# Column halves in the last matmul chain of an attention and mixture kernel, a last weight in four pieces, and short products between the weights

## The chip, the cores and the metric

The kernel runs on one core of a Trainium2 chip. The metric is the device time of one execution in microseconds. A core has a matrix engine (TensorE, PE in the profile), which writes its products into PSUM banks, a vector engine (VectorE, DVE), a scalar engine (ScalarE, ACT), a third elementwise engine (GpSimd, POOL), and a sync engine (SyncE, SP), from which this kernel issues every transfer between device memory (DRAM) and the on-chip memory. All of them run on their own and wait for each other by semaphores; each takes its own instructions strictly in the order in which they were written.

## What is computed

Cut to what matters (the inputs are float32; the norm guards of 1e-9 are left out here):

```python
a      = softmax(phi, axis=memories)          # 8 batches, 8 heads, 576 positions, 32 memories
k_m    = einsum('bhsm,bhsd->bhmd', a, k)      # keys and values pooled into 32 memories
v_m    = einsum('bhsm,bhsd->bhmd', a, v)
x      = softmax(q @ k_m.T / 8) @ v_m         # as rows: 4608 x 512
logits = x @ moe_phi                          # 4608 x 32 slots
slot_input = softmax(logits, axis=rows).T @ x # 32 x 512, four slots for each of 8 experts
for e in range(8):
    h = relu(slot_input[e] @ w1[e])           # first layer:  4 x 512 @ 512 x 1024
    slot_out[e] = h @ w2[e]                   # second layer: 4 x 1024 @ 1024 x 512
out = softmax(logits, axis=slots) @ slot_out  # 4608 x 512
```

The change touches the second layer, the sum that follows it, and the first rows of the last product.

## The kernel before

Until about two thirds of the time the kernel works on attention: four pairs of batches, one after another, whose logits are kept, and whose slot inputs are added up. When the last pair is done, the slot inputs are scaled into the tile `SIM` (L1000), and the mixture begins.

**First layer.** `expert_in` multiplies each expert's slot inputs with its `w1`, which arrives as two transfers of 1 MB. Four experts share a PSUM bank, and four products of 32 columns of the array each run side by side (`tile_position`). After four experts `hidden` applies the relu (L1080), turns the result by two transposes (L1089) and stores it as `hT` (L1095).

**Second layer.** `expert_out` takes each `w2` as two transfers of 1 MB, called halves here: 16 halves in all. A half is four products with 512 columns each (L1113), again side by side on four quarters of the array. All 64 products add up in one accumulator, `pacc`, in the first bank of the pair `kvbank`. The four quarters hold partial sums over different hidden units.

**Slot weights of the rows.** Between the second layer's products `slots` computes, for each of the four pairs of batches, the softmax of the logits over the slots on DVE and ACT (L1136 to L1159), and PE turns them in groups of three by transposes (L1170) into `cT`, which ACT stores (L1175).

**Slot sums.** DVE copies `pacc` out of PSUM (L1194). One product with `rep`, four identities side by side, adds the four quarters (L1199). ACT stores the result rounded to the fast matmul format as `sr` (L1204), and DVE puts the rounding remainder into the lower 64 rows (L1207). So `sr` is ready after five steps in a row.

**Output.** 36 groups of 128 rows follow, each one product of a `cT` block with `sr` (L1220), copied out of PSUM by ACT (L1229) and DVE (L1231) in turn. Three groups fill a tile `ot`, which one transfer of 768 KB writes to `out` (L1239), twelve transfers in all. There are six `ot` tiles.

**What sets the order.** Every step is recorded with `add(engine, cost, function, r=reads, w=writes)`. `Plan.order` simulates the five engines and the transfers with these costs in microseconds and writes the instructions in the order that comes out; the waits between engines are then derived from what each instruction really reads and writes in memory, not from `r` and `w`. A tile's place in memory comes from a pool (`Slots`); the 19 places of `ws` hold the weights, so that the last 13 of the 32 weight transfers reuse places that the first layer has read.

Of the kernel before, what the change touches and what calls it, by code (L numbers as in the profile page):

```python
# [8 lines left out]
F32 = mybir.dt.float32  # L9
F32R = mybir.dt.float32r  # L10
AF = mybir.ActivationFunctionType
ALU = mybir.AluOpType
# [4 lines left out]
PE, DVE, ACT, POOL, SP = range(5)  # L17
# [3 lines left out]
class Plan:  # L21
# [23 lines left out]
    def add(self, eng, cost, fn, r=(), w=(), also=(), pri=None, dma=0.0, slack=0.0):  # L45
        i = len(self.ops)
        deps = set()
        tiles = {}
        for x in r:
            for key in x:  # L50
                tiles[key[0]] = None
                if key in self.last_w:
                    deps.add(self.last_w[key])
        for x in w:
            for key in x:
                tiles[key[0]] = None
                if key in self.last_w:
                    deps.add(self.last_w[key])
                deps.update(self.reads.get(key, ()))
        for x in w:  # L60
            for key in x:
                self.last_w[key] = i
                self.reads[key] = []
        for x in r:
            for key in x:
                self.reads.setdefault(key, []).append(i)
        deps.discard(i)
        tiles = [t for t in tiles if t.pool is not None]
        for t in tiles:
            t.users += 1  # L70
        need = tiles + [t for t in also if t not in tiles]
        if pri is None:
            pri = self.phase[0]
            self.phase[0] += self.phase[1]
        self.ops.append((eng, cost, fn, deps, pri, dma, tiles, need, slack))
# [156 lines left out]
def dve(n):  # L232
    return 0.15 + n / 960.0


def act(n, psum=True):
    return (0.16 if psum else 0.19) + n / 1200.0
# [6 lines left out]
def pe(n, cols, cnt, passes=2, tiles=1):  # L244

    return n * max(0.0185, (cols / 1200.0 + cnt * passes / 2400.0) / tiles)
# [6 lines left out]
def kernel(  # L253
# [24 lines left out]
    nc = tc.nc  # L278
    B, H, S, D = q.shape
    M = phi.shape[3]  # L280
    E, DM, FF = w1.shape
    NS = moe_phi.shape[1]
    SE = NS // E
    P = 128
    HALF = 64
    J = S // HALF
# [14 lines left out]
    add = plan.add  # L301
# [6 lines left out]
    def keep(name, shape, dtype=F32, parts=1):  # L308
        return Tile(ap=const.tile(shape, dtype, name=name), parts=parts)
# [3 lines left out]
    b_kv = Slots([kvbank])  # L313
    b_m = Slots(banks[:3], [(i, 1) for i in range(3)])
    b_l = Slots(banks[3:], [(3, 1)])
    scbank = psum.tile([P, 2, 512], F32, name="scbank")
    b_s2 = Slots([scbank])
    b_o = Slots(banks, [(i, 1) for i in range(4)], (b_m, b_l))
# [38 lines left out]
    def stack(shape, n, fifo=False):  # L357
# [43 lines left out]
    rep_b = keep("rep", [P, 4, NS])  # L401
    ones_b = keep("ones", [P, P])
    mphd_b = keep("mphd", [P, C, 2, NS])
    ident, maskhp, maskc, rep, ones, mphd = (
        x.ap for x in (ident_b, maskhp_b, maskc_b, rep_b, ones_b, mphd_b)
    )
# [49 lines left out]
    def load(dst, src, nbytes, w, pri=None):  # L456
        add(
            SP, 0.06, lambda: nc.sync.dma_start(dst(), src), w=[w],
            dma=nbytes / DMA_RATE, pri=pri,
        )  # L460
# [580 lines left out]


    EG = 4
    hTb = hTs.tile().split(E // EG)
    hT = lambda: hTb.ap.rearrange("p (x y) -> p x y", x=8)
    add(POOL, 2.0, lambda: nc.gpsimd.memset(hTb.ap, 0.0), r=[SIM], w=[hTb])

    def load_w(src):
        t = ws.tile()
        load(lambda: t.ap.rearrange("p (a x) -> p a x", a=src.shape[1]), src, 1 << 20, t)  # L1050
        return t

    pacc = b_kv.tile()

    def expert_in(e, hb):
        w1v = w1[e].rearrange("(c p) f -> p c f", p=P)
# [44 lines left out]

    def expert_out(e):
        w2v = w2[e].rearrange("(j p t) d -> p j (t d)", j=4, t=2)
        w2b = [load_w(w2v[:, 2 * i: 2 * i + 2]) for i in range(2)]
        for i in range(2):

            def f(i=i):
                wv = w2b[i].ap.rearrange("p (j t d) -> p j t d", j=2, t=2)
                for t in range(2):
                    for j in range(2):  # L1110

                        x = 2 * t + j
                        nc.tensor.matmul(  # L1113
                            pacc.ap[NS * x: NS * x + NS, 0, :DM],
                            hT()[:, 4 * t + 2 * i + j, NS * e: NS * e + NS],
                            wv[:, j, t, :],
                            start=(e == 0 and i == 0),
                            stop=(e == E - 1 and i == 1),
                            tile_position=(0, NS * x),
                        )  # L1120

            add(PE, pe(8, NS, DM, tiles=4), f, r=[hTb.part(e // EG), w2b[i]], w=[pacc])


    cmxs = sb("cmx", [P, J], 1)
# [1 line left out]
    cT = {}  # L1127
# [56 lines left out]
    for e in range(E):  # L1184
        expert_out(e)
        if e % 2 == 1:
            slots(e // 2)


    accs, sr = acs.tile(), keep("sr", [P, DM], dtype=F32R)  # L1190
    outv = out.rearrange("(p j) d -> p j d", j=J)
    so = b_m.tile()
    add(
        DVE, dve(DM), lambda: nc.vector.tensor_copy(accs.ap, pacc.ap[:, 0, :DM]),  # L1194
        r=[pacc], w=[accs],
    )
    add(
        PE, 1.2,
        lambda: nc.tensor.matmul(  # L1199
            so.ap[:, :DM], rep.rearrange("p a n -> p (a n)"), accs.ap, start=True, stop=True  # L1200
        ),
        r=[accs, rep_b], w=[so],
    )
    add(ACT, act(DM), lambda: nc.scalar.copy(sr.ap, so.ap[:, :DM]), r=[so], w=[sr])  # L1204
    add(
        DVE, dve(DM),
        lambda: nc.vector.tensor_tensor(  # L1207
            sr.ap[HALF:], so.ap[HALF:, :DM], sr.ap[HALF:].bitcast(F32), op=ALU.subtract
        ),
        r=[so, sr], w=[sr],  # L1210
    )
    for bp in range(NBP):
        for j0 in range(0, J, G):
            ot = ots.tile().split(G)
            for i in range(G):
                t = bp * J + j0 + i
                po = b_o.tile()
                add(
                    PE, 0.33,
                    lambda po=po, i=i, ct=cT[bp, j0]: nc.tensor.matmul(  # L1220
                        po.ap[:, :DM], ct.ap()[:, i * P: i * P + P], sr.ap, start=True, stop=True
                    ),
                    r=[sr, cT[bp, j0]], w=[po], also=[ot],
                )

                def f(po=po, ot=ot, i=i, t=t):
                    dst = ot.ap[:, i * DM: i * DM + DM]
                    if t % 2 == 0:
                        nc.scalar.copy(dst, po.ap[:, :DM])  # L1229
                    else:  # L1230
                        nc.vector.tensor_copy(dst, po.ap[:, :DM])  # L1231

                add(
                    *((ACT, act(DM)) if t % 2 == 0 else (DVE, dve(DM))), f,
                    r=[po], w=[ot.part(i)],
                )
            add(
                SP, 0.06,
                lambda bp=bp, j0=j0, ot=ot: nc.sync.dma_start(  # L1239
                    outv[bp * P: bp * P + P, j0: j0 + G, :],  # L1240
                    ot.ap.rearrange("p (g d) -> p g d", g=G),
                ),
                r=[ot], dma=P * G * DM * 4 / DMA_RATE,
            )
# [31 lines left out]
```

## Time and profile before

| | |
|---|---|
| median of 3 runs | 223.73 us (223.68 to 225.53) |
| the profiled execution, own time | 221.83 us |
| its span, first to last instruction | 220.1 us |
| granted TensorE clock, mean over the span | 0.916 of full speed |
| read from and written to DRAM | 66.65 MB and 9.44 MB |
| PE busy | 172.5 us of the span, 78% |
| DVE busy | 135.5 us, 62% |
| POOL busy | 86.7 us, 39% |
| ACT busy | 71.4 us, 32% |

The profile is one execution on the chip. Its views give busy times by engine, a chain of waits (the work that ended last, followed back from the end), groups of instructions, a timeline, and sums over chosen stretches. All times in it are microseconds from the span's start. L1113 is line 1113 of the kernel. PEld is the loading of weights into the array, which overlaps the products; a float32 product that is not a transpose leaves two records of each kind, so that the 64 products of L1113 stand as 128. Matmuls are pipelined: the duration of one record holds the way through the array, so the price of a row of them is the distance from start to start, not the mean of one. An execution takes a little longer than its span: 221.83 - 220.1 = 1.7 us here.

### The profile page before, as it was taken

The page shows a single profiled execution, that of the slowest core. Times are in us where ns is not written, and L with a number is a line of the kernel's source. Part 1 is how long each engine was busy: PE and PEld are TensorE (multiplying, and loading weights), DVE is VectorE, ACT ScalarE, POOL GpSimd, SP SyncE. Part 2 cuts the span into 40 slices and gives each one's busy share as a digit, 9 for nine tenths or more (in the row PEclk, how much of TensorE's full clock was granted, in tenths as well). Part 3 has the DMA queues.
Part 4 walks back from the last instruction along what each step waited for, and adds up shares of the span by engine and source line. Part 5 has one row for each costly group of instructions (what it writes and reads, how often), then busy time and mean ns, then how long its engine had stood idle before and what let it go on. Part 6 is the DMA issues. An engine that isn't in the chain of part 4 may idle for free.

```text
span 220.1 us, 5624 instructions
## 1 busy us (share of the span) xinstructions
PE 172.5 (78%) x2418; PEld 105.3 (48%) x2418; DVE 135.5 (62%) x230; ACT 71.4 (32%) x182; POOL 86.7 (39%) x85
## 2 busy tenths in 40 slices
PE   8997977695798988598988799629999975599400
PEld 6676745354564654356654387415554340065100
DVE  6825048969459999879658965499102860268500
ACT  2041234542516626337342340201002331168400
POOL 6298019596934992999623641030000000000000
PEclk9999999979699999999969999976999999769755
DMA  6999999999999999999596493999999998049997
GB/s 215 383 395 390 380 392 381 390 380 390 385 388 389 388 406 380 389 392 406 194 410 212 188 420 102 401 350 327 395 413 410 408 409 320 3 179 411 415 415 295
DMA packets 27881, 76.45 MB, mean 347 GB/s; under 512 B 1744, under 2 KB 5840, under 8 KB 27856
## 3 DMA queue, kind: packets, MB, share of 16 engines
q1 hardware_dynamic: 27856, 76.09, 91.1%
q8 instruction: 19, 0.31, 0.6%
q14 instruction: 6, 0.05, 0.1%
HBM read 66.65 MB, written 9.44 MB: 346 GB/s over the span
## 4 chain that ended last, share of the span: by engine, by line
PE 41%; DMA 22%; DVE 14%; POOL 9%; issue 5%; ACT 2%; SPq 1%; DVEq 0%; POOLq 0%
DMA top<-in_q_dram 10%; DMA arena<-in_moe_w_dram 9%; PE bank L1064 7%; PE kvbank L476 6%; PE bank L785 5%; PE scbank L716 4%; PE bank L1220 4%; PE kvbank L599 3%; DMA out_dram<-arena 3%; DVE arena L700 3%; POOL arena L774 3%; POOL arena L562 3%; PE bank L849 2%; PE kvbank L1113 2%; POOL arena L751 2%
## 5 line engine op out<-in xcount | busy, mean ns | idle before, releaser
L549 POOL TENSOR_TENSOR arena<-arena 128x1152 f32<-128x1152 f32 x8 | 21.0, 2632 | 16.0 <-ACT arena L544 13.3
L476 PE MATMUL kvbank<-ones 128*128 128x256 f32 x92 | 25.4, 419 | 2.2 <-ACT arena L622 1.1
L700 DVE STREAM_TRANSPOSE arena<-top 128x1152 f32<-128x1152 f32 x16 | 21.7, 1361 | 7.1 <-DMA top<-in_q_dram 7.1
L774 POOL TENSOR_TENSOR arena<-arena,ssm 128x576 f32<-128x576 f32 x16 | 18.5, 1162 | 15.6 <-DVE ssm L770 15.5
L562 POOL TENSOR_TENSOR arena<-arena 128x128 f32<-128x128 f32 (+2 forms) x32 | 23.4, 731 | 2.3 <-ACT arena L555 0.3
L716 PE MATMUL scbank<-arena 64*64 64x288 f32 x256 | 21.6, 433 | 3.0 <-DVE arena L730 2.5
L785 PE MATMUL bank<-arena 128*128 128x288 f32 x64 | 21.4, 464 | 2.6 <-DVE arena L777 2.6
L751 POOL TENSOR_TENSOR arena<-arena,smx 128x576 f32<-128x576 f32 x16 | 18.4, 1158 | 11.5 <-DVE smx L746 11.5
L599 PE MATMUL kvbank<-arena 64*32 64x128 f32 x1152 | 20.2, 273 | 2.2 <-issue 1.5
L476 PEld LDWEIGHTS kvbank<-ones 128*128 128x128 f32 x92 | 18.1, 207 | 6.7 <-issue 1.6
L511 DVE TENSOR_REDUCE arena<-arena 128x128 f32<-128x1152 f32 x8 | 17.0, 2138 | 5.6 <-DMA arena<-in_phi_dram 5.6
L599 PEld LDWEIGHTS kvbank<-arena 64*32 64x32 f32 x1152 | 16.2, 106 | 6.3 <-issue 3.9
L1064 PE MATMUL bank<-arena,SIM 128*32 128x256 f32 x256 | 16.4, 421 | 3.4 <-DVE SIM L1000 3.4
L1113 PE MATMUL kvbank<-arena 128*32 128x512 f32 x128 | 15.6, 598 | 2.9 <-DMA arena<-in_moe_w_dram 2.9
L730 DVE STREAM_TRANSPOSE arena<-scbank 128x576 f32<-128x576 f32 x16 | 12.2, 765 | 8.9 <-PE scbank L716 8.9
L785 PEld LDWEIGHTS bank<-arena 128*128 128x128 f32 x64 | 12.1, 206 | 8.1 <-DVE arena L777 3.8
L1220 PE MATMUL bank<-sr,cT 128*128 128x512 f32 x36 | 13.2, 505 | 3.1 <-DVE sr L1207 1.4
L1231 DVE COPY arena<-bank 128x512 f32<-128x512 f32 x18 | 11.8, 691 | 4.7 <-DMA out_dram<-arena 2.4
L777 DVE STREAM_TRANSPOSE arena<-arena 128x576 f32<-128x576 f32 x16 | 12.1, 758 | 3.8 <-POOL arena L774 3.7
L716 PEld LDWEIGHTS scbank<-arena 64*64 64x64 f32 x256 | 9.0, 137 | 10.8 <-DVE arena L730 4.5
L756 ACT ACTIVATE arena<-arena 128x576 f32<-128x576 f32 x16 | 11.0, 688 | 8.4 <-POOL arena L751 8.4
L1064 PEld LDWEIGHTS bank<-arena,SIM 128*32 128x32 f32 x256 | 8.6, 121 | 10.7 <-DVE SIM L1000 3.6
(104 smaller groups left out, 234.4 us busy)
## 6 DMA issues: line engine op xcount, KB each, us to landing
arena<-in_moe_w_dram SPq DMA_DIRECT2D x32, 1024.0 KB, 9.9
top<-in_q_dram SPq DMA_DIRECT2D x8, 1152.0 KB, 13.8
arena<-in_k_dram SPq DMA_DIRECT2D x8, 1152.0 KB, 11.2
arena<-in_v_dram SPq DMA_DIRECT2D x8, 1152.0 KB, 13.6
out_dram<-arena SPq DMA_DIRECT2D x12, 768.0 KB, 7.6
arena<-in_phi_dram SPq DMA_DIRECT2D x8, 576.0 KB, 8.7
arena<-in_moe_phi_dram SPq DMA_DIRECT2D x1, 64.0 KB, 4.8
```

The lines of the kernel that those rows point to most:

```text
L476: lambda: nc.tensor.matmul(warm.ap, ones, ones.unsqueeze(1).to_broadcast([P, 2, P]), start=True, stop=True,),
L549: lambda: nc.gpsimd.tensor_tensor(ph(), ph(), mb.ap.unsqueeze(2).to_broadcast([P, C, J, M]), op=ALU.subtract),
L562: plus = lambda o, x, y: nc.gpsimd.tensor_tensor(o, x, y, op=ALU.add)
L599: nc.tensor.matmul(acc.ap[M * c: M * c + M, a, : 2 * D], ph()[h0: h0 + HALF, c, j, :], kv()[h0: h0 + HALF, :, c, j * D: j * D + D], start= ...
L700: nc.vector.transpose(qT.ap.rearrange("p (i u y) -> p u i y", i=2, y=Y), qt.ap[:, h * QT_SZ: h * QT_SZ + QT_SZ].rearrange("p (u i x) -> p ...
L716: nc.tensor.matmul(scb.ap[HALF * g: HALF * g + HALF, a, :JY], kb[g].ap[h0: h0 + HALF, i, c].rearrange("p r m -> p (r m)"), qT[g][c // 2].a ...
L751: lambda: nc.gpsimd.tensor_tensor(exv(), exv(), bc(mx), op=ALU.subtract),
L774: lambda: nc.gpsimd.tensor_tensor(exv(), exv(), bc(sm), op=ALU.mult),
L785: nc.tensor.matmul(lp.ap[:, :JY], vpb.ap[:, h, :], aT.ap[:, a * JY: (a + 1) * JY], start=(h == 0), stop=(h == H - 1),)
L1064: nc.tensor.matmul(hb.ap[NS * j: NS * j + NS, :256], SIM.ap[:, 2 * i + c, NS * e: NS * e + NS], wv[:, c, 256 * j: 256 * j + 256], start=(e ...
L1113: nc.tensor.matmul(pacc.ap[NS * x: NS * x + NS, 0, :DM], hT()[:, 4 * t + 2 * i + j, NS * e: NS * e + NS], wv[:, j, t, :], start=(e == 0 an ...
L1220: lambda po=po, i=i, ct=cT[bp, j0]: nc.tensor.matmul(po.ap[:, :DM], ct.ap()[:, i * P: i * P + P], sr.ap, start=True, stop=True),
```

## The change

The accumulator `pacc` now has two parts: columns 0 to 255 in the first bank of `kvbank`, columns 256 to 511 in the second. Each half of a `w2` is eight products with 256 columns in place of four with 512: first the four of the lower columns (d = 0), then the four of the upper ones (d = 1).

The last half of the last `w2` is read by four transfers of 256 KB, each with 1 KB runs, in place of one of 1 MB with 4 KB runs: two for the lower columns, then two for the upper ones. After each of the other 15 halves, `warmup` adds three products of a 128x128 matrix of ones with itself into a bank of `scbank` that nothing reads.

The slot sums are done once for each column half; the copy out of the accumulator is done by DVE for the lower half and by ACT for the upper. The first three row groups are computed in column halves too, three products for the lower and three for the upper half, and each of these groups is written by a transfer of its own (256 KB with 2 KB runs). The other 33 groups are as before, so there are 14 output transfers.

The core of the diff:

```diff
+    WARM_E = 3
...
-    pacc = b_kv.tile()
+    pacc = b_kv.tile().split(2)
+    HD = DM // 2
+    coolb = b_s2.tile()
+
+    def warmup(n, r=()):
+        for _ in range(n):
+            add(
+                PE, 0.22,
+                lambda: nc.tensor.matmul(
+                    coolb.ap[:, 0, :P], ones, ones, start=True, stop=True,
+                ),
+                r=[ones_b, *r], w=[coolb],
+            )
...
-        w2b = [load_w(w2v[:, 2 * i: 2 * i + 2]) for i in range(2)]
+        w2h = w2[e].rearrange("(j p t) d -> p j t d", j=4, t=2)
         for i in range(2):
...
+            if e < E - 1 or i == 0:
+                load(
+                    lambda t=t: t.ap.rearrange("p (a x) -> p a x", a=2),
+                    w2v[:, 2 * i: 2 * i + 2], 1 << 20, t,
+                )
+            else:
+                t.split(4)
+                for d in range(2):
                     for j in range(2):
...
+                        load(
+                            lambda d=d, j=j, wide=wide: wide()[:, j, :, d * HD: d * HD + HD],
+                            w2h[:, 2 * i + j, :, d * HD: d * HD + HD], 1 << 18, t.part(2 * d + j),
                         )
...
+            for d in range(2):
+
+                def f(i=i, d=d, wide=wide):
+                    for t in range(2):
+                        for j in range(2):
+
+                            x = 2 * t + j
+                            nc.tensor.matmul(
+                                pacc.ap[NS * x: NS * x + NS, d, :HD],
+                                hT()[:, 4 * t + 2 * i + j, NS * e: NS * e + NS],
+                                wide()[:, j, t, d * HD: d * HD + HD],
+                                start=(e == 0 and i == 0),
+                                stop=(e == E - 1 and i == 1),
+                                tile_position=(0, NS * x),
+                            )
...
+            if t.parts == 1:
+                warmup(WARM_E, [t])
...
+    for d in range(2):
+        x = slice(d * HD, d * HD + HD)
+        so = b_m.tile()
+        if d == 0:
+            add(
+                DVE, dve(HD), lambda x=x, d=d: nc.vector.tensor_copy(accs.ap[:, x], pacc.ap[:, d, :HD]),
+                r=[pacc.part(d)], w=[accs.part(d)],
+            )
+        else:
+            add(
+                ACT, act(HD), lambda x=x, d=d: nc.scalar.copy(accs.ap[:, x], pacc.ap[:, d, :HD]),
+                r=[pacc.part(d)], w=[accs.part(d)],
+            )
...
+    for d in range(2):
+        if d == 0:
+            ot0 = ots.tile().split(2 * G)
+        x = slice(d * HD, d * HD + HD)
+        for i in range(G):
+            po = b_o.tile()
...
+            if d == 1:
+                add(
+                    SP, 0.06,
+                    lambda i=i: nc.sync.dma_start(
+                        outv[:P, i, :], ot0.ap[:, i * DM: i * DM + DM],
+                    ),
...
     for bp in range(NBP):
-        for j0 in range(0, J, G):
+        for j0 in range(0 if bp else G, J, G):
```

Three places show what becomes of the order. The first is PE at the end of the second layer, in the rows of before from the last-but-one visit of transposes on; `kvbank<-arena` are the layer's products, `bank<-ident,arena` the transposes, `bank<-arena,rep` the slot sums and `bank<-sr,cT` the output products:

```order
L1170 MATMUL bank_62<-ident,arena 128x128 x3
L1113 MATMUL kvbank<-arena 32x512 x4
L1170 MATMUL bank_63<-ident,arena 128x128 x3
L1170 MATMUL bank_64<-ident,arena 128x128 x3
L1170 MATMUL bank_62<-ident,arena 128x128 x3
L1113 MATMUL kvbank<-arena 32x512 x16
L1199 MATMUL bank_63<-arena,rep 128x512
L1220 MATMUL bank_65<-sr,cT 128x512
```

The same place in the changed kernel, with the products of ones as `scbank<-ones`:

```order
L1142 MATMUL kvbank<-arena 32x256 x8
L1062 MATMUL scbank<-ones 128x128 x3
L1205 MATMUL bank_64<-ident,arena 128x128 x3
L1205 MATMUL bank_62<-ident,arena 128x128 x3
L1142 MATMUL kvbank<-arena 32x256 x8
L1062 MATMUL scbank<-ones 128x128 x3
L1142 MATMUL kvbank<-arena 32x256 x8
L1062 MATMUL scbank<-ones 128x128 x3
L1142 MATMUL kvbank<-arena 32x256 x4
L1242 MATMUL bank_63<-arena,rep 128x256
L1142 MATMUL kvbank<-arena 32x256 x4
L1242 MATMUL bank_64<-arena,rep 128x256
```

The three products of ones stand behind each half; the transposes now stand directly behind such a group; and the slot sum of the lower columns stands ahead of the last four products of the upper ones. The first group of ones, that of the first half, was moved ahead of the whole first layer. No product of ones waits for a transfer, since it reads nothing but the ones.

Before, the last product of the attention (L909) is followed directly by the first layer on PE. In the changed kernel this stands there:

```order
L909 MATMUL bank_63<-arena 64x128 x4
L1062 MATMUL scbank<-ones 128x128 x3
L1078 MATMUL bank_62<-arena,SIM 32x256 x64
L1078 MATMUL bank_64<-arena,SIM 32x256 x8
L1103 MATMUL bank_63<-ident,arena 128x128 x2
L1078 MATMUL bank_64<-arena,SIM 32x256 x56
```

One group of ones has come in between; the first layer itself (L1064, now L1078) keeps its order. The third place is DVE after the second layer, in the changed kernel, up to the first tiles that are written out:

```order
L1232 COPY arena<-kvbank 128x256
L1253 TENSOR_TENSOR sr<-bank_63,sr 64x256
L1277 COPY arena<-bank_62 128x256
L1253 TENSOR_TENSOR sr<-bank_64,sr 64x256
L1277 COPY arena<-bank_65 128x256
L1277 COPY arena<-bank_63 128x256
```

One copy for the lower columns of the output (L1277, bank_62) stands ahead of the remainder of the upper ones (L1253, bank_64), on which the rest waits. ACT has its six steps of the same kind in between: the cast of the lower `sr`, the copy of the upper accumulator half, the cast of the upper `sr`, then three output copies.

More of the change, by code (lines that the diff above doesn't have):

```diff
@@ L1103, in expert_out @@
         w2v = w2[e].rearrange("(j p t) d -> p j (t d)", j=4, t=2)
-        w2b = [load_w(w2v[:, 2 * i: 2 * i + 2]) for i in range(2)]
+        w2h = w2[e].rearrange("(j p t) d -> p j t d", j=4, t=2)
         for i in range(2):
-            def f(i=i):
-                wv = w2b[i].ap.rearrange("p (j t d) -> p j t d", j=2, t=2)
-                for t in range(2):
-                    for j in range(2):
[L1112 to L1119, printed above, removed]
-                        )
-            add(PE, pe(8, NS, DM, tiles=4), f, r=[hTb.part(e // EG), w2b[i]], w=[pacc])
+            t = ws.tile()
+            wide = lambda t=t: t.ap.rearrange("p (j t d) -> p j t d", j=2, t=2)
+            if e < E - 1 or i == 0:
[6 more added lines that the diff above has]
+                for d in range(2):
+                    for j in range(2):
+                        load(
+                            lambda d=d, j=j, wide=wide: wide()[:, j, :, d * HD: d * HD + HD],
+                            w2h[:, 2 * i + j, :, d * HD: d * HD + HD], 1 << 18, t.part(2 * d + j),
+                        )
+            for d in range(2):
[12 more added lines that the diff above has]
+                add(
+                    PE, pe(4, NS, HD, tiles=4), f,
+                    r=[hTb.part(e // EG), *((t.part(2 * d), t.part(2 * d + 1)) if t.parts > 1 else [t])],
+                    w=[pacc.part(d)],
+                )
+            if t.parts == 1:
+                warmup(WARM_E, [t])
@@ L1187 @@
             slots(e // 2)
-    accs, sr = acs.tile(), keep("sr", [P, DM], dtype=F32R)
+    accs, sr = acs.tile().split(2), keep("sr", [P, DM], dtype=F32R, parts=2)
     outv = out.rearrange("(p j) d -> p j d", j=J)
[L1192 to L1211, printed above, removed]
+    for d in range(2):
[10 more added lines that the diff above has]
+                r=[pacc.part(d)], w=[accs.part(d)],
+            )
+        add(
+            PE, 0.5,
+            lambda x=x, so=so: nc.tensor.matmul(
+                so.ap[:, :HD], rep.rearrange("p a n -> p (a n)"), accs.ap[:, x], start=True, stop=True
+            ),
+            r=[accs.part(d), rep_b], w=[so],
+        )
+        add(
+            ACT, act(HD), lambda x=x, so=so: nc.scalar.copy(sr.ap[:, x], so.ap[:, :HD]),
+            r=[so], w=[sr.part(d)],
+        )
+        add(
+            DVE, dve(HD),
+            lambda x=x, so=so: nc.vector.tensor_tensor(
+                sr.ap[HALF:, x], so.ap[HALF:, :HD], sr.ap[HALF:, x].bitcast(F32), op=ALU.subtract
+            ),
+            r=[so, sr.part(d)], w=[sr.part(d)],
+        )
@@ new lines, with f @@
+    for d in range(2):
[4 more added lines that the diff above has]
+            po = b_o.tile()
+            add(
+                PE, 0.22,
+                lambda po=po, i=i, x=x, ct=cT[0, 0]: nc.tensor.matmul(
+                    po.ap[:, :HD], ct.ap()[:, i * P: i * P + P], sr.ap[:, x], start=True, stop=True
+                ),
+                r=[sr.part(d), cT[0, 0]], w=[po], also=[ot0],
+            )
+            def f(po=po, i=i, d=d):
+                dst = ot0.ap[:, i * DM + d * HD: i * DM + d * HD + HD]
+                if i % 2 == d:
+                    nc.scalar.copy(dst, po.ap[:, :HD])
+                else:
+                    nc.vector.tensor_copy(dst, po.ap[:, :HD])
+            add(
+                *((ACT, act(HD)) if i % 2 == d else (DVE, dve(HD))), f,
+                r=[po], w=[ot0.part(2 * i + d)],
+            )
+            if d == 1:
+                add(
+                    SP, 0.06,
+                    lambda i=i: nc.sync.dma_start(
+                        outv[:P, i, :], ot0.ap[:, i * DM: i * DM + DM],
+                    ),
+                    r=[ot0.part(2 * i), ot0.part(2 * i + 1)], dma=P * DM * 4 / DMA_RATE,
+                )
```

## The prediction

> **What bounds the kernel now.** I read the slices of the page first, to see where the transfers stop:
>
> ```profile
> PE   8997977695798988598988799629999975599400
> ...
> PEclk9999999979699999999969999976999999769755
> DMA  6999999999999999999596493999999998049997
> GB/s 215 383 395 390 380 392 381 390 380 390 385 388 389 388 406 380 389 392 406 194 410 212 188 420 102 401 350 327 395 413 410 408 409 320 3 179 411 415 415 295
> ```
>
> A slice is 5.5 us. From the 25th on the transfers run at about 410 GB/s; then comes a hole, the 34th to 36th slice (320, 3, 179 GB/s), with a lowered PE clock beside it, and after it the output at 411 to 415 GB/s. The hole lies between the last weight and the first output. The chain of waits (start, length, what) says what fills it:
>
> ```profile
> 168.59 18.81 DMA arena<-in_moe_w_dram
> ...
> 187.44 1.11 PE kvbank L1113 x8
> 188.58 0.70 DVE arena L1194
> ...
> 189.41 1.76 PE bank L1199 x2
> ...
> 191.20 0.59 ACT sr L1204
> ...
> 191.82 0.70 DVE sr L1207
> ...
> 192.57 7.80 PE bank L1220 x21
> 200.37 7.29 DMA out_dram<-arena
> ```
>
> The weights are bound by transfers: the last was issued at 168.59 and landed at 187.40. Then the last half of the second layer and the five steps of the slot sums run one after another. So two things count: when the last products of L1113 start (187.44), and how long it takes from there to the first output transfer. That one is issued at 194.87, by the timeline:
>
> ```profile
> 193.40 0.59 ACT L1229 COPY arena<-bank 128x512 f32<-128x512 f32 x1 [1.61 <-PE bank L1220]
> 193.83 0.69 DVE L1231 COPY arena<-bank 128x512 f32<-128x512 f32 x1 [1.31 <-PE bank L1220]
> ...
> 194.87 14.57 SPq L1239 DMA_DIRECT2D out_dram<-arena  x12
> ```
>
> That is 7.43 us. What follows is bound by transfers again, and the rest of the time hangs on 194.87. The stretches show PE in the meantime (columns: length, busy time with instructions of PE, PEld, DVE, ACT, POOL, granted clock, DMA share, GB/s):
>
> ```profile
> 145.40:152.20 6.80, 4.53 (x44) 2.17 (x48) 6.40 (x16) 0.44 (x1) 0.99 (x1) 0.50 0.96 329
> ...
> 164.20:183.50 19.30, 18.16 (x154) 6.84 (x146) 9.47 (x24) 6.23 (x15) 0.00 (x0) 1.00 1.03 409
> 183.50:187.44 3.94, 1.06 (x8) 0.16 (x8) 0.00 (x0) 0.00 (x0) 0.00 (x0) 1.00 0.61 242
> 187.44:194.87 7.43, 5.12 (x15) 2.22 (x16) 2.27 (x4) 1.76 (x3) 0.00 (x0) 0.65 0.01 2
> 194.87:218.50 23.63, 10.91 (x32) 5.59 (x30) 10.91 (x17) 9.04 (x16) 0.00 (x0) 0.72 0.98 399
> ```
>
> This is the row that decides: from 164.20, where the second layer begins, PE is busy for 18.16 of 19.30 us. It starts late, with a heap of landed weights, and only catches up with the transfers at 183.50. Up to 187.44 it is busy 18.16 + 1.06 = 19.2 of 23.2 us, so 4.0 us are free.
>
> **The products of ones.** Each has two records. These rows price a visit to such products:
>
> ```profile
> 158.14 6.25 PE L1064 MATMUL bank<-arena,SIM 128*32 128x256 f32 x112
> 165.55 2.78 PE L1113 MATMUL kvbank<-arena 128*32 128x512 f32 x24
> 172.97 1.20 PE L1170 MATMUL bank<-ident,arena 128*128 128x128 f32 x9
> 176.15 0.84 PE L1170 MATMUL bank<-ident,arena 128*128 128x128 f32 x6
> 176.93 1.07 PE L1113 MATMUL kvbank<-arena 128*32 128x512 f32 x8
> 177.93 0.55 PE L1170 MATMUL bank<-ident,arena 128*128 128x128 f32 x3
> ```
>
> Three float32 products of 128x128 with 128 columns are six records of the shape of the transposes, and the row with six took 0.84 us (0.78 from its start to that of the next products). The nearest other rows bound it: twelve records of ones with 256 columns took 2.79 us, so half of one six times is 0.70; the visit of three records, which is mostly coming and going, took 0.55, twice that is 1.10.
>
> ```profile
> 131.07 2.79 PE kvbank L476 x12
> ```
>
> I take 0.84, the same count and shape. One of the 15 groups falls in PE's idle time ahead of the first layer (below); 14 x 0.84 = 11.8 us fall into the second layer (9.8 to 15.4). They wait for nothing, and behind each stand the next half's products, so all of it is PE's time.
>
> **The halves in columns.** Sixteen records of 256 columns replace eight of 512. The same shape in the first layer cost 6.25 / 112 = 0.0558 a record, 0.89 a half; now it is 2.78 / 24 x 8 = 0.93. Fifteen halves: -0.5. The transposes' five visits now join a visit of ones; what they save is the 0.55 of three records less three at 1.20 / 9, 0.15 each: -0.75. DVE and ACT, which make the transposes' input, get more time.
>
> **When the last products start.** 164.2 + 19.2 + 11.8 - 0.5 - 0.75 = 193.95, against 187.44: 6.5 us later. PE never waits for a weight again. The four pieces land long before that, whatever they cost; uncovered, they would cost the gap between the rate with short runs and that of the weights, by this stretch of phi's 1152-byte runs 359 against 409 GB/s, so 2.9 in place of 2.6 us for the megabyte:
>
> ```profile
> 3.00:6.00 3.00, 3.00 (x10) 2.44 (x9) 2.32 (x5) 0.00 (x0) 1.34 (x3) 1.00 1.11 359
> ```
>
> SP issues three transfers more there; its weight transfers wait for the first layer's reads and run 18.8 us ahead of landing, so these issues are hidden.
>
> **From there to the first output.** Prices: four 256-column products 8 x 0.0558 = 0.45; to their reader 1.14 - 0.93 = 0.21 (187.44 to 188.58, less the half); back to PE 0.13 (189.28 to 189.41). The copies with 256 columns:
>
> ```profile
> 157.12 0.38 ACT L1080 ACTIVATE arena<-bank 128x256 f32<-128x256 f32 x1 [3.93 <-PE bank L1064]
> ...
> 158.32 0.29 DVE L1095 COPY arena<-bank 128x128 f32<-128x128 f32 x1 [3.69 <-PE bank L1089]
> ```
>
> ACT 0.38 as it stands; DVE 0.42, a third of the way from 0.29 (128) to 0.69 (512). A slot sum with 256 columns has two records like those of L476, 2 x 0.23 = 0.46. With zero at the start of the lower columns' products: DVE copies 0.66 to 1.08, PE sums 1.21 to 1.67; only then, for PE takes its rows in order, do the upper columns' products run, to 2.12; ACT casts 1.88 to 2.26, DVE takes the remainder to 2.70. ACT copies the upper columns 2.33 to 2.71, PE sums to 3.30, ACT casts 3.51 to 3.89. The upper remainder waits on DVE for the output copy ahead of it (3.8 to 4.22), and ends at 4.64. The next output product gives DVE's copy at 5.05 to 5.47, and SP issues the first 256 KB at 5.50. Against 7.43: -1.9. If the clock drops in it, PE's four steps of about 0.45 double, and a gain of 0.1 is left; more than 2.5 would need nearly all hops gone. Between these I keep the sum of the rows.
>
> **The output.** Three transfers of 256 KB at 0.64 us each (410 GB/s) cover the 2 us in which ACT and DVE copy three groups at 0.59 and 0.69. Their 2 KB runs cost at most phi's ratio, 0.1 for each: +0.2, bounds 0 and +0.3. The 33 other groups keep their rows.
>
> **Sum.** 6.5 - 1.9 + 0.2 = +4.8 us. On the profiled execution 221.83 + 4.8 = 226.6. The median of the runs shown is 1.9 higher, 223.73; nothing says where these 1.9 lie, and the second layer is a tenth of the span, so I add to the median: 228.5.
>
> **Rivals.** *The clock holds in the first layer.* It is at 0.50 from 145.40 to 152.20, so the first layer, from 147.67 on, runs at half speed up to there and loses 2.3 us. What goes ahead:
>
> ```profile
> 141.93:145.34 3.41, 1.55 (x16) 1.20 (x15) 2.16 (x4) 0.19 (x1) 0.96 (x1) 1.00 0.97 375
> ...
> 143.60 0.66 PE L909 MATMUL bank<-arena 128*64 128x128 f32 x8 [0.78 <-DVE arena L890]
> 147.67 1.08 PE L1064 MATMUL bank<-arena,SIM 128*32 128x256 f32 x8 [3.40 <-DVE SIM L1000]
> ...
> 187.44:189.70 2.26, 1.35 (x9) 0.46 (x10) 0.69 (x1) 0.00 (x0) 0.00 (x0) 1.00 0.00 0
> 189.70:196.50 6.80, 5.40 (x11) 2.90 (x10) 2.88 (x5) 2.84 (x5) 0.00 (x0) 0.50 0.13 54
> ```
>
> The first group of ones fills 0.84 of the 3.40 idle. If that keeps the clock up, the second layer starts 2.3 earlier, and since PE now bounds it, all of it comes through: 226.2. Against it: 2.6 us stay idle, and the clock fell at 189.70 after idle pieces of PE that were all shorter: of 183.50 to 187.44 it was busy 1.06 us, in two waits of about 1.4 each, and 0.9 us lie between 188.5 and 189.41. The Trainium skill ("TensorE: Matmul & The Clock Gate", section "Why this matters for your kernels") asks only for no idle gap beyond about 3 us. By that rule this rival would hold, and 226.2 would be the sum. The trace does not agree, since the drop at 189.70 came with shorter gaps.
>
> *The ones hide in waits.* Then the two lower pieces landing at 187.40 - 2.6 + 1.45 = 186.3 set the start, the upper products at 186.3 + 1.7 find theirs, and the first output goes at 186.3 + 5.5 = 191.8: -3.1 + 0.2 = -2.9, 220.8, faster. It decides from the point where 14 groups fit into the 4.0 us that are free, at 0.29 us a group; no row is under 0.70. A start of the second layer 6.5 us earlier would do it too, but that hangs on `SIM` at 147.6.
>
> *The output starves.* If small transfers do not follow each other closely, the output's start has holes; one hole of the length of a piece, 0.64, gives 229.1. Against it, the last weight stood 18.8 us behind others of 2.6 us each, and there was no hole between them.
>
> **Chances.** The forecast 0.64; the clock holds 0.19; the ones hide 0.07; the output starves 0.10. One per cent, 2.2 us, is about what a measurement tells from no change. Holding clock and the low price of 0.70 together give 4.8 - 2.3 - 2.0 = +0.5, within it: that is 0.12 of the 0.19. So faster 0.07, same 0.12, slower 0.81. The range goes from 225.5, the holding clock with a price a little under 0.84, to 230.5, a group at about 0.98 us.
>
> **What would show it.** Right: 90 records of ones, 84 of them after 164; no wait of the second layer's products for a weight; the last ones at about 194; two slices without transfers; 5.5 us from there to the first output. Wrong: waits for weights at the end of the second layer, or a full clock at 148.

## The result and the profile after

The changed kernel took 231.61 us (median of 4 runs, 231.21 to 233.43) beside 224.63 us of the kernel before (4 runs, 223.68 to 227.23). The ratio is 1.0345, 95% interval 1.0294 to 1.0397: slower, as forecast, but by 7.7 us at 224 where 4.8 were forecast, and above the range. The ratio is not that of the two medians, since executions in a slower state of the chip, here the one of 227.23 us, are left out of it.

The slices of the page, of the changed kernel (span 229.4 us, so a slice is 5.7 us):

```profile
PE   8998987765989975999897996499999999788400
...
PEclk9999999997699999799889999769999999999755
DMA  6999999999999999997776939999999970059994
GB/s 216 388 392 390 381 389 383 386 384 390 381 396 381 400 399 385 393 369 289 281 277 187 384 156 371 343 342 360 415 408 408 407 251 3 0 212 415 407 418 197
```

The hole between the last weight and the first output is now three slices wide (251, 3, 0), and PE is at nine tenths in the first two of them: what the transfers wait for is PE. The chain of waits (start, length, what) from the end of the second layer on:

```profile
191.50 0.86 PE scbank L1062 x6
192.37 0.66 PE bank L1205 x6
193.02 1.00 PE kvbank L1142 x16
194.02 0.86 PE scbank L1062 x6
194.89 1.00 PE kvbank L1142 x16
195.89 0.86 PE scbank L1062 x6
196.75 0.61 PE kvbank L1142 x8
...
197.39 0.43 DVE arena L1232
...
197.96 0.67 PE bank L1242 x2
198.63 0.61 PE kvbank L1142 x8
...
199.27 0.38 ACT arena L1237
...
199.69 0.70 PE bank L1242 x2
...
200.67 0.42 DVE arena L1277
...
201.12 0.44 DVE sr L1253
...
201.70 0.59 PE bank L1266 x3
```

No weight stands in it any more. Halves (L1142) and ones (L1062) follow each other without a gap up to 196.7; then comes the new chain of slot sums. The same in stretches (length, busy time of PE, PEld, DVE, ACT, POOL, granted clock, DMA share, GB/s):

```profile
165.31:196.68 31.37, 31.25 (x366) 20.66 (x358) 9.46 (x24) 6.34 (x15) 0.00 (x0) 1.00 0.73 284
196.68:202.58 5.90, 3.77 (x29) 1.96 (x28) 2.19 (x6) 2.04 (x6) 0.00 (x0) 1.00 0.00 0
202.58:226.00 23.42, 11.13 (x32) 5.41 (x32) 11.24 (x18) 9.04 (x17) 0.00 (x0) 0.77 0.98 396
226.00:229.40 3.40, 0.00 (x0) 0.00 (x0) 0.00 (x0) 0.00 (x0) 0.00 (x0) 0.50 0.12 51
```

The first row is the second layer up to its last products, the second the chain to the first output transfer (issued at 202.58), the other two the output. Against the profiled execution of before:

| stretch | before | changed | difference | forecast |
|---|---|---|---|---|
| start to second layer | 164.21 | 165.31 | +1.1 | 0 |
| second layer up to the last products | 23.23 | 31.37 | +8.1 | +6.5 |
| last products to first output transfer | 7.43 | 5.90 | -1.5 | -1.9 |
| first output transfer to the end | 25.2 | 26.8 | +1.6 | +0.2 |
| whole | 220.1 | 229.4 | +9.3 | +4.8 |

The first row is not the change's: in the profiles of all kernels below the first layer starts between 147.7 and 153.0, and in that of before at the early end of it; in the eight kernels below that have no group of ones ahead of it, the start lies between 147.7 and 149.6. The other three add up to +8.2, or 3.7% of 221.83, within the interval of the ratio.

### The profile page after: what moved, and what is told of

It is laid out like the page before. It is cut to its first block, busy times and chain, and to the rows that moved or that the text cites. A ratio compares the mean times of both kernels' runs of the same rounds, so it can differ in the third digit from the quotient of the medians.

```text
span 229.4 us, 6089 instructions
## 1 busy us (share of the span) xinstructions
PE 186.0 (81%) x2641; PEld 121.2 (53%) x2641; DVE 135.8 (59%) x233; ACT 71.5 (31%) x185; POOL 86.6 (38%) x85
## 4 chain that ended last, share of the span: by engine, by line
PE 60%; DMA 17%; DVE 15%; issue 1%; ACT 1%; SPq 1%; DVEq 0%
DMA top<-in_q_dram 9%; PE bank L1078 7%; PE kvbank L1142 7%; PE bank L785 7%; PE kvbank L599 6%; PE kvbank L476 6%; PE scbank L716 5%; PE scbank L1062 5%; DMA out_dram<-arena 4%; DMA arena<-in_phi_dram 3%; PE bank L849 3%; DVE arena L700 3%; DVE arena L511 3%; PE bank L1299 2%; DVE arena L730 2%; PE bank L1205 2%
## 5 line engine op out<-in xcount | busy, mean ns | idle before, releaser
L476 PE MATMUL kvbank<-ones 128*128 128x256 f32 x92 | 26.0, 428 | 2.2 <-ACT arena L622 1.1
L599 PE MATMUL kvbank<-arena 64*32 64x128 f32 x1152 | 21.9, 291 | 1.9 <-issue 1.2
L716 PE MATMUL scbank<-arena 64*64 64x288 f32 x256 | 20.6, 417 | 3.0 <-DVE arena L730 2.5
L599 PEld LDWEIGHTS kvbank<-arena 64*32 64x32 f32 x1152 | 17.6, 112 | 6.0 <-issue 3.8
L1078 PE MATMUL bank<-arena,SIM 128*32 128x256 f32 x256 | 16.7, 426 | 2.5 <-DVE SIM L1000 2.5
L1142 PE MATMUL kvbank<-arena 128*32 128x256 f32 x256 | 17.1, 385 | 0.0
L1299 PE MATMUL bank<-sr,cT 128*128 128x512 f32 x33 | 11.5, 463 | 4.1 <-ACT arena L1308 3.0
L1062 PEld LDWEIGHTS scbank<-ones 128*128 128x128 f32 x90 | 11.2, 191 | 5.5 <-issue 5.5
L1310 DVE COPY arena<-bank 128x512 f32<-128x512 f32 x17 | 11.1, 687 | 5.0 <-DMA out_dram<-arena 4.9
L1062 PE MATMUL scbank<-ones 128*128 128x128 f32 x90 | 13.9, 291 | 0.0
```

Source lines behind the costliest of these rows:

```text
L476: lambda: nc.tensor.matmul(warm.ap, ones, ones.unsqueeze(1).to_broadcast([P, 2, P]), start=True, stop=True,),
L599: nc.tensor.matmul(acc.ap[M * c: M * c + M, a, : 2 * D], ph()[h0: h0 + HALF, c, j, :], kv()[h0: h0 + HALF, :, c, j * D: j * D + D], start= ...
L716: nc.tensor.matmul(scb.ap[HALF * g: HALF * g + HALF, a, :JY], kb[g].ap[h0: h0 + HALF, i, c].rearrange("p r m -> p (r m)"), qT[g][c // 2].a ...
L1062: lambda: nc.tensor.matmul(coolb.ap[:, 0, :P], ones, ones, start=True, stop=True,),
L1078: nc.tensor.matmul(hb.ap[NS * j: NS * j + NS, :256], SIM.ap[:, 2 * i + c, NS * e: NS * e + NS], wv[:, c, 256 * j: 256 * j + 256], start=(e ...
L1142: nc.tensor.matmul(pacc.ap[NS * x: NS * x + NS, d, :HD], hT()[:, 4 * t + 2 * i + j, NS * e: NS * e + NS], wide()[:, j, t, d * HD: d * HD + ...
```

## The experiments

The theory was that the ones fill a PE that has no room for them in the second layer. What else the change does could then be told apart only without them.

**1. No ones at all.**

```diff
-    WARM_E = 3
+    WARM_E = 0
```

> All products of ones are taken out of the changed kernel; all else stays. Theory (the ones fill PE's time in the second layer, and that is the whole loss): the last products start again when their weight lands, about 186.5 us where the first layer starts at 147.7, and the first output is issued 5.9 to 6.4 us after that, about 2 us earlier than the 194.87 of before; with 0.2 to 1.6 us lost in the output the ratio to before is 0.990 to 0.998. Rival (the split products, the pieces or the small transfers lose as well): ratio 1.00 or more, with PE busy or waiting between the halves where it was not before.

Measured: ratio 0.9917, interval 0.9864 to 0.9970; 223.08 beside 223.90 us. The second layer takes 22.4 us up to its last products, and these wait for their weight again. So the whole loss hangs on the ones, and the rest of the change is a small gain. Its chain took 6.44 us, because the lower products had to wait for the second of their two pieces in the middle, and its output 26.1.

**2. The ones alone in the kernel before.** `coolb` and `warmup` are added as in the change.

```diff
...
             add(PE, pe(8, NS, DM, tiles=4), f, r=[hTb.part(e // EG), w2b[i]], w=[pacc])
+            if 2 * e + i < 2 * E - 1:
+                warmup(3, [w2b[i]])
```

> The kernel before with three products of ones after each of 15 halves, nothing else changed. Theory: 14 groups of 0.98 us less some 4 us that were free, so the last products start 8 to 9 us later than 187.44, and the chain of slot sums runs at full clock, 0.5 us shorter: ratio 1.034 to 1.040. Rival (the loss comes from the split products): ratio under 1.015.

Measured: ratio 1.0222, interval 1.0165 to 1.0280. That lies between the two, 0.012 under the theory's 1.034 and 0.007 above the rival's 1.015: the ones alone lose 2.2%, but not the whole 3.45%. The second layer takes 30.3 us up to the last products (at 195.5), one less than with the column halves; the old chain takes 6.28 in place of 7.43, at full clock; the output takes 25.2. From half to half it is 1.86 us, as in the full change (1.87), so the halves in columns cost PE nothing more and save it nothing. Two differences explain the smaller loss in the profiles. The second layer is shorter because the order puts the last nine transposes (about 1 us) behind the last products, where PE waits for the copy of the accumulator; and the output lacks the 1.6 us of experiment 5.

**3. One product of ones in place of three.**

```diff
-    WARM_E = 3
+    WARM_E = 1
```

> The changed kernel with one product of ones after each half in place of three. Theory with the price by records (0.11 each plus about 0.3 for the change of the array's shape): a visit costs 0.54 in place of 0.98, the last products start 6 us earlier than in the changed kernel, ratio to before 1.005 to 1.010. Rival (a visit costs the same however many products it has): the start moves by under 2 us, ratio 1.025 or more. Rival (only the records cost): a visit is 0.22, the start falls back to the weight's landing, ratio under 1.0.

Measured: ratio 1.0062, interval 1.0017 to 1.0107, as the price by records has it. The timeline of this kernel (start, length), two halves with a visit in between:

```profile
167.72 1.07 PE L1142 MATMUL kvbank<-arena 128*32 128x256 f32 x16
168.72 0.49 PE L1062 MATMUL scbank<-ones 128*128 128x128 f32 x2
169.14 1.07 PE L1142 MATMUL kvbank<-arena 128*32 128x256 f32 x16
```

And of the changed kernel, with three products:

```profile
168.19 1.07 PE L1142 MATMUL kvbank<-arena 128*32 128x256 f32 x16
169.19 0.94 PE L1062 MATMUL scbank<-ones 128*128 128x128 f32 x6
170.06 1.07 PE L1142 MATMUL kvbank<-arena 128*32 128x256 f32 x16
```

From half to half it is 1.42 us with two records and 1.87 with six: 0.11 a record. A half takes 0.89 by the first layer's rows, so a visit costs 0.53 and 0.98, of which 0.31 are coming and going, however many products it has. Four quarters of 32 columns and the whole array alternate there. The Trainium skill ("TensorEngine Tiling (Array Packing)", section "Key Properties") says that a change of the tiling mode drains the engine. The 0.31 us agree with that, but no run here shows that the drain is what they are spent on.

**4. Ones only where PE waits.**

```diff
-            if t.parts == 1:
+            if t.parts == 1 and 2 * e + i >= 2 * E - 3:
                 warmup(WARM_E, [t])
```

> The changed kernel with products of ones only after the last two of the 15 halves, where PE waits for weights. Theory: they fit into the waits and cost nothing; if the clock falls without them in the last chain (as at 189.70 before), they hold it and the ratio is 0.002 to 0.004 under that of the kernel without any ones; if the clock does not fall there without them, the ratio is the same. Rival (any product of ones ahead of the last weight delays it): above the kernel without ones by 0.004 or more.

Measured: ratio 0.9928, interval 0.9887 to 0.9969; the kernel without ones had 0.9917. They bring nothing that shows, and cost little: from the first record of the last-but-one half to the last one of the lower products it is 2.13 us here (185.75 to 187.88) and 1.70 in experiment 1 (187.10 to 188.80), so the last group held the lower products up by some 0.4 us, too little for the ratios. In the profiles the clock stayed full through the chain with them and without them.

**5. Without the first group of ones.**

```diff
-            if t.parts == 1:
+            if t.parts == 1 and e + i > 0:
                 warmup(WARM_E, [t])
```

> The changed kernel without the first of its 15 groups of ones, the one in PE's idle time ahead of the first layer. Theory on the output (one of the 16 KB reads of PE's instructions, which come every 250 records or so, falls into the output stage, and its transfer engine ends late): with 12 records fewer the last of these reads falls off the end, and from the first output's issue to the end it takes 25.3 us in place of 26.8; ratio about 1.028. Rival (the 256 KB transfers with 2 KB runs cost it): still 26.8, ratio 1.034. On the clock: the first layer has its 6.8 us of half clock with the group and without it; if the group mattered, the second layer would start later here by up to 2 us.

Measured: ratio 1.0263, interval 1.0190 to 1.0337. The stretches of its profile:

```profile
164.39:195.76 31.37, 31.25 (x366) 20.66 (x358) 9.46 (x24) 6.34 (x15) 0.00 (x0) 1.00 0.72 278
195.76:201.65 5.89, 3.76 (x29) 1.95 (x28) 2.19 (x6) 2.04 (x6) 0.00 (x0) 1.00 0.00 0
201.65:225.07 23.42, 10.80 (x32) 5.19 (x32) 11.26 (x18) 9.07 (x17) 0.00 (x0) 0.76 0.98 397
225.07:226.94 1.87, 0.00 (x0) 0.00 (x0) 0.00 (x0) 0.00 (x0) 0.00 (x0) 0.50 0.19 76
```

Second layer and chain are those of the changed kernel to the hundredth. The output is cut after 23.42 us in both; what follows takes 1.87 us in place of 3.40. The rows of the queues say what is gone, first the changed kernel, then this one:

```profile
q8 instruction: 21, 0.34, 0.6%
```

```profile
q8 instruction: 20, 0.33, 0.6%
```

One read of instructions. In the trace such a read is one packet of 16 KB, comes once in some 250 records of PE on average (products and weight loads counted), and takes about 1 us (0.88 to 1.38). In the changed kernel the last of them stands at 213.8, amid the output. Every output transfer lands in 16 parts. Up to 211.77 the sixteen parts of each lie within 0.2 us; from the transfer whose first fifteen land at 213.45 to 213.66 on, the last part comes 1.5 to 2.2 us after the fifteenth, down to the last transfer (226.93 and 228.43). Without the first group all sixteen lie within 0.3 us to the end. The 1.6 us of the output stage are this, and not the small transfers. Why a read of 0.94 us leaves a part that is 2.2 us late is not shown.

**6. The ones at the end, in the kernel before.** `coolb` and `warmup` are added here too.

```diff
...
+            if 2 * E - 3 <= 2 * e + i < 2 * E - 1:
+                warmup(3, [w2b[i]])
```

> The kernel before with products of ones only after the last two of the 15 halves, nothing else. Theory (more than half of what the changed chain gained is the clock): the ones hold the clock, the old chain of slot sums takes 6.3 us in place of 7.4, the start of the last products stays: ratio 0.993 to 0.997. Rival (the gain came from the column halves): the chain stays above 7 us, ratio 1.0.

Measured: ratio 0.9987, interval 0.9944 to 1.0030: no gain to be seen, a miss. The last products began at 188.32, the chain took 6.77 us, between the 6.3 of the theory and the 7 of the rival, and the clock fell in the midst of it, at 192.6. So ones ahead of the old chain did not hold the clock in it. Its own long waits are the likely reason, since PE has one product between 189.4 and 192.8; no run shows it by itself.

**7. The last weight in one piece.** From the kernel of experiment 4, so with ones at the end; as both column halves then arrive together, the upper products stand directly behind the lower ones on PE. The edit against the changed kernel:

```diff
-            if e < E - 1 or i == 0:
+            if True:
                 load(
...
-            if t.parts == 1 and 2 * e + i >= 2 * E - 3:
+            if 2 * E - 3 <= 2 * e + i < 2 * E - 1:
                 warmup(WARM_E, [t])
```

> The kernel with ones at the end only, but the last weight in one transfer of 1 MB, and the upper products directly behind the lower ones on PE. Theory (the pieces bring nothing, since PE sums the lower columns before it multiplies the upper ones and the short runs land 0.5 us later): the last products start 0.5 us later, the chain takes 4.6 us in place of 5.9, ratio 0.004 below that of the kernel with the pieces, about 0.989. Rival (the early lower pieces carry the gain): ratio 0.003 or more above it.

Measured: ratio 0.9897, interval 0.9855 to 0.9939; chain 4.66 us.

**8. The pieces, with the upper products first.** From experiment 4 as well; the edit also gives the first output copies of the lower columns to ACT and those of the upper ones to DVE:

```diff
-                    r=[hTb.part(e // EG), *((t.part(2 * d), t.part(2 * d + 1)) if t.parts > 1 else [t])],
+                    r=[hTb.part(e // EG), *((t.part(0), t.part(1)) if t.parts > 1 else [t])],
...
-                if i % 2 == d:
+                if d == 0:
                     nc.scalar.copy(dst, po.ap[:, :HD])
...
-                *((ACT, act(HD)) if i % 2 == d else (DVE, dve(HD))), f,
+                *((ACT, act(HD)) if d == 0 else (DVE, dve(HD))), f,
```

> The kernel with ones at the end only, with the four pieces, but the upper products directly behind the lower ones on PE, and the first row groups' copies by ACT for the lower and DVE for the upper columns, so that no output copy stands ahead of the upper remainder. Theory: the chain waits for the upper pieces, 1.6 us after the lower ones, and takes 5.1 us in place of 5.9: ratio 0.003 to 0.004 below that of the kernel with ones at the end. Rival (the order on PE did not matter): the same ratio.

Measured: ratio 0.9891, interval 0.9828 to 0.9953; chain 5.06 us. The chain is 0.8 shorter than in experiment 4, as expected, and with the whole weight 1.2 shorter, but there it starts later. Counted from the start of the last-but-one half, which waits for its weight in all of them, to the first output it is 7.32 us in experiment 1, 7.76 in 4, 7.15 in 7 and 6.93 here. The ratios lie together. So four pieces and one do nearly the same for the time, and the order of the changed kernel, with the sums of the lower columns ahead of the products of the upper ones and an output copy ahead of the upper remainder, took back what the early pieces gave; which of the two orders matters more was not separated.

**9. Nine ones ahead of the first layer.** The group that experiment 5 took out comes back with nine products.

```diff
+    warmup(9, [sip])
     for g in range(E // EG):
         hb = b_m.tile()
...
-            if t.parts == 1:
+            if t.parts == 1 and e + i > 0:
                 warmup(WARM_E, [t])
```

> The changed kernel with nine products of ones in place of three ahead of the first layer, where PE idles; they leave about 1.2 us idle in place of 2.5. Theory on the clock (it falls by the busy share of a window of 3.4 us, not by a single long gap): the window is now busy enough, the clock stays full over the first layer, which takes 14.3 us from its first product to the second layer in place of 16.8, and all 2.3 us come through: ratio 1.024. Rival: the clock falls all the same, 16.8 us, ratio 1.034. Theory on the output: with 24 records more than in the changed kernel the last read of PE's instructions lies in the output stage again, which takes 26.3 us or more from the first issue; rival: 25.3 as in the kernel without the first group.

Measured: ratio 1.0242, interval 1.0173 to 1.0312. On the output the theory holds: there are 21 reads of instructions again, the last at 212.0, and the stage takes 26.7 us; from the transfer after the read on, the last part of each lands 1.3 to 1.9 us late. On the clock nothing is settled. In this profile, whose execution took 233.11 us where the other three took 228.8 to 230.5, it had already fallen at 142.09, ahead of the group:

```profile
142.09:152.33 10.24, 9.01 (x68) 7.08 (x46) 5.35 (x14) 1.61 (x7) 2.02 (x1) 0.50 0.75 264
152.33:167.34 15.01, 15.01 (x265) 8.99 (x267) 5.24 (x15) 0.83 (x2) 0.00 (x0) 1.00 0.99 379
```

The first layer then ran at full clock, in 14.3 us, but it started only at 153.0:

```profile
149.42 3.65 PE L1062 MATMUL scbank<-ones 128*128 128x128 f32 x18
153.00 7.98 PE L1078 MATMUL bank<-arena,SIM 128*32 128x256 f32 x144
```

The steps ahead had run at half clock, yet `SIM` was ready at 150.66. From there on the first layer waited another 2.3 us for the ones, which took 3.6 us, most of it at half clock, and stand ahead of it on PE. So in this execution they cost what the full clock was to save. The ratio is the expected one, but not for the expected reason as far as this profile shows, and it can't be told from that of experiment 5.

**10. Halves for the slot sums, not for the row groups.** From experiment 7, with the loop over the first three row groups in halves left out:

```diff
-        for j0 in range(0 if bp else G, J, G):
+        for j0 in range(0, J, G):
```

> The kernel with ones at the end only and the last weight in one piece, but without the column halves of the first three row groups: all twelve output transfers have 768 KB again. Theory (the halves of the slot sums and the small first transfers gain separately): the first output waits for three copies of 512 columns, the chain takes 5.4 to 5.6 us in place of 4.66, the output 25.15: ratio 0.003 to 0.004 above that of the kernel with the row groups in halves. Rival (the gain is all in the slot sums): the same ratio.

Measured: ratio 0.9916, interval 0.9878 to 0.9954; chain 5.37 us, output 25.2. The chain is 0.7 longer, as expected, and the small transfers cost under 0.1 in the output (25.23 in experiment 7, 25.18 here). The ratios can't be told apart.

**11. The same without ones.** From experiment 7, with the call of `warmup` left out.

> The kernel with the last weight in one piece and the upper products directly behind the lower ones, and no products of ones at all. Theory: where the clock falls in the last chain, its PE steps double and it takes 5.2 to 5.6 us in place of 4.66; ratio 0 to 0.004 above that of the kernel with ones at the end, depending on the window's place in each run. Rival (the ones at the end cost as much as they bring): the same or a lower ratio.

Measured: ratio 0.9866, interval 0.9805 to 0.9927: below the 0.9897 with ones, as the rival has it, though the intervals overlap. In its profile the clock did fall, from 189.5 on, and the chain took 5.79 us. Its rows beside those of experiment 7, first without ones:

```profile
187.97 1.11 PE kvbank L1142 x16
189.11 0.44 DVE arena L1230
...
189.68 1.21 PE bank L1240 x2
...
190.91 0.38 ACT sr L1246
...
191.32 0.44 DVE sr L1251
...
191.80 1.90 PE bank L1264 x6
```

```profile
191.30 1.11 PE kvbank L1142 x16
...
192.44 0.44 DVE arena L1232
...
193.01 0.68 PE bank L1242 x2
```

The slot sums (L1240, L1242) take 1.21 at the lower clock and 0.68 at the full one. So a fall of the clock costs this chain 1.1 us in all. Whether the ones at the end prevent it is not shown: the clock stayed full without them in experiment 1 and fell in spite of them in experiment 6, and the medians show no gain.

The kernels with column halves and without ones among the first 13 halves (experiments 1, 4, 7, 8, 10 and 11) are all faster than both kernels compared here, than that of before by 0.7 to 1.3%. The lowest ratio has that of experiment 11: column halves, the last weight in one piece, no ones, 221.83 beside 224.30 us.

## Why the prediction was wrong in size

**PE takes over as the bound.** Right, and shown by experiments 1 to 3: without ones no loss is left, with them alone 2.2% are lost, the loss grows with their records, and PE is busy for 31.25 of 31.37 us. The weights, the four pieces among them, have all landed by 189 and are waited for by nobody.

**The price of a visit**, "I take 0.84, the same count and shape". This term was too small: it is 0.98. The row of six transposes was the right one, but I read its length from its own first record; the 0.1 us between the end of the half and that record is lost too, and the row doesn't hold it. Over 14 visits that makes 2.0 us, where the second layer went 1.6 beyond the forecast. Two other terms were off as well. The 0.5 that the halves in columns were to save did not come (1.86 and 1.87 us from half to half). The five visits of transposes that joined a visit of ones saved more: if each saves the coming and going, 0.31 in place of 0.15, that is an estimated 0.8. Together 2.0 + 0.5 - 0.8 = 1.7. The upper bound of the price, 1.10, held, and the price alone would have left the time inside the range, whose upper end was worked out with 0.98.

**The chain**, 5.50 forecast, 5.90 measured, step for step as written: the sums at 1.28 and 3.01 after the start in place of 1.21 and 2.84, the upper remainder at 4.44 in place of 4.22, behind the output copy as forecast. But the credit went to the wrong part: of the 1.5 us gained on 7.43, experiment 2, with the old chain at full clock, gives 1.15 to the clock and leaves 0.4 to the halves. That the halves gain more with another order (a chain of 4.66 with the whole weight, 5.06 with the pieces) was not seen.

**The output**, "+0.2, bounds 0 and +0.3": this term failed, +1.6, and it is what carried the time beyond the range. Its own step was right, since the small transfers cost 0.1 (25.2 to 25.35 us with them, 25.2 without, where no read stands in the output). What was left out is that 113 more products, which leave 446 more records with their weight loads, also need more instructions read, and that one of these reads would fall into the one stage that transfers bound. The profile of before has 19 such reads, and none was priced.

**The holding clock.** It fell at 146.75 in spite of the first group, with 2.53 us idle, and it was low on some stretch between 140 and 155 in every profile of the study. The rule of the Trainium skill ("TensorE: Matmul & The Clock Gate", section "Why this matters for your kernels"), no gap beyond about 3 us, did not keep it: in the changed kernel the stretch 143.33 to 146.75 had PE busy for no more than 1.83 of 3.42 us by the modelled ends, and the clock fell after it:

```profile
143.33:146.75 3.42, 1.83 (x17) 1.36 (x16) 2.76 (x4) 0.18 (x1) 1.56 (x1) 1.00 0.96 329
146.75:153.57 6.82, 5.09 (x48) 2.33 (x52) 6.35 (x18) 0.46 (x2) 0.46 (x1) 0.50 0.94 347
```

**The base.** I added to the median of three runs, 223.73. That was near enough: with more runs beside the experiments the kernel before had medians of 223.9, 225.4 and 224.3.

**A reading.** "From the 25th on the transfers run at about 410 GB/s" is not what the slices show: the 25th has 102, the next four 401, 350, 327 and 395, and about 410 begins with the 30th. No term rests on it.

**What stays open.** Whether enough ones ahead of the first layer hold the clock there was not settled (experiment 9), and there they delayed it. What places the clock's low stretches, and whether they alone move the start of the first layer, is not known. In the profiles of experiments 1, 4, 7, 8, 10 and 11 the second layer starts between 164.2 and 166.5, and their ratios lie closer together than that, so that these kernels can't be put in an order by them.

## What to carry to other kernels

Before work is put into an engine "while it waits", count its free time in that very stretch, not over the span: PE was 78% busy on the page and had 4 us left where 13.7 were added. Price a visit of other work from the last row ahead of it to the first row behind it, and ask what its instructions cost where they are read. And when a chain is split in two for overlap, look at the in-order queue: one row of the first half ahead of one of the second can take back what the split gave.

## What the hardware showed that was not expected

Reads of PE's own instructions, 16 KB each, one in some 250 records, take about 1 us of transfer time, and one of them in the last, transfer-bound stage holds back one of the sixteen parts of every output transfer behind it and makes the end 1.5 us later (26.8 and 26.7 us with it, 25.2 to 25.35 without it in the kernel before and nine others; 26.1 in experiment 1, whose last read, at 194.5, met the first output, of which the last part landed 0.9 us late). Twelve records fewer put it away.

The clock changes only at steps of 3.41 us: the low stretches were 3.4, 6.8, 10.2 or 13.7 us long in all thirteen profiles, apart from the one that runs to the end, and begin at points that differ between executions (140.6 to 146.8 us for the one around the start of the first layer). The Trainium skill ("TensorE: Matmul & The Clock Gate", section "What's actually happening") has a free-running window of 3.41 us, and the trace agrees with that.
